# A decode kernel whose first loads are split over two DMA queues, and the same kernel with all loads on one

## The chip, the cores and the metric

The kernel runs on one core of one Trainium2 chip. The metric is the device time of one execution in microseconds, the median of several runs. A change of some microseconds out of 194 is what this case is about.

## The reference, cut to what matters

One token `x` (1 x 512) is normalised and goes into two branches. Branch A is attention over the last 4096 positions of a cache with 32 heads of 128; branch B is a small MLP. The output is `x + A * silu(B)`.

```python
xn = layernorm(x)
# A
q = xn @ wq                                   # 512 -> 32 heads x 128
k, v = k_cache[:, :, -4096:], v_cache[:, :, -4096:]
p = softmax((q . k) * 128 ** -0.5)
s = (p . v) @ wo                              # 4096 -> 512
# B (one token, so the shifted groups of gelu(...) are all zero)
x1 = xn + hs                                  # hs = 0 @ w2
g = silu(x1 + gelu(layernorm(x1) @ w3) @ w4)
return x + s * g
```

All tensors are bfloat16. The keys and the values are 33.6 MB each, wq and wo 4.19 MB each, w3 and w4 1.41 MB each, w2 0.52 MB; x is 1 KB.

## The kernel before, in words

The 32 heads are worked in eight groups of four (`G = 4`). A group's keys are one load of 4.19 MB (4096 KB in the profile's units: 128 partitions of 32 KB), its values another. `load()` (line 76) issues a load on SP's queue and keeps program order there; SP does nothing else. `load_kv` (lines 95 to 101) takes the next buffer of a pool and loads keys or values, in cuts where it is given some. Keys have three buffers, values two; a load waits on SP until the buffer's former contents have been read, and everything behind it on SP's queue waits with it.

The first part of the kernel, up to line 303, is the preparation. The layer norm of x is made from `x_bf` (x as 128 x 4, line 78); `x_row` (x as four rows, on partitions 0, 32, 64 and 96, line 80) serves the end of branch B (`xn_row`, line 242) and the last addition (line 653). The query weights `wq_sb` give the query in 32 matmuls (line 208), from which ScalarE and TensorE make the two forms that the groups use: `q_bc`, a row over all partitions (lines 214 and 216), and `q_pair`, columns (lines 221 and 225). Branch B is w2 (line 233, on zeros), w3 (20 matmuls of line 252 into `a_ps`), the gelu on ScalarE (`a_row`, line 255), a turn (`at_ps`, line 258; `a_bf`, line 260), w4 (lines 263 and 270 into `hr_ps`), VectorE's copy `hr` (line 273), the fold `h2_ps` (lines 275 and 276), `bv` on VectorE (line 278) and the silu (line 280). A scheduler orders this part on each engine by its own estimates, so an edit of the loads can change the order on TensorE, VectorE and ScalarE.

In the order of issue, ScalarE's queue has `x_bf`, `x_row` and wq; SP's has w2, w3, w4 in two pieces, then the keys.

The second part is a loop over `s` whose order on TensorE, VectorE and ScalarE is that of the program text (`manual_schedule`, line 527). In step `s` the keys of group `s` are worked and the values of group `s - 2`. Of a group's 128 key rows per partition, VectorE does 64 or 80 (`k_vector`, lines 317 to 323: a product `prod`, line 321, and a sum into `S`, line 323, in four parts); TensorE does the others (transposes, line 339, copied by ScalarE, line 342, then the scores, line 350). Softmax runs one step later; the values are wide matmuls (line 427), the last group's last cut a chain of 32 (line 461). The weights' pool `wts` is given back at `s == 2` (line 536) and its room becomes the values' buffers, so the first value load waits until the weights have been read. At the end, `wo` is applied in blocks (lines 518 and 155), and lines 651 to 654 make and store the output row (`out_row`, four partitions).

Of the kernel before, what the change touches and what calls it, by code (L numbers as in the profile page):

```python
# [8 lines left out]
P = 128  # L9
BF16 = mybir.dt.bfloat16  # L10
# [16 lines left out]
def kernel(  # L27
# [14 lines left out]
    nc = tc.nc  # L42

    Bb, Sq, D = A_x.shape
# [9 lines left out]
    KC = D // P  # L54
# [18 lines left out]
    wts = wts_guard.__enter__()  # L73

    def load(dst, src):
        return tc.keep_in_program_order(nc.sync.dma_start(out=dst, in_=src))  # L76

    x_bf = small.tile([P, KC], BF16, name="x_bf")
    nc.scalar.dma_start(out=x_bf[:], in_=A_x.rearrange("a b (p c) -> p (a b c)", p=P))
    x_row = small.tile([P, P], BF16, name="x_row")  # L80
    nc.gpsimd.memset(x_row[:], 0.0)
    nc.scalar.dma_start(out=x_row[0:P:32, :], in_=A_x.rearrange("a b (j n) -> (a b j) n", j=KC))
    wq_sb = wts.tile([P, KC, HD], BF16, name="wq_sb")
    nc.scalar.dma_start(out=wq_sb[:].rearrange("p c n -> p (c n)"),
                        in_=A_wq.rearrange("(a b c) n -> b a (c n)", a=4, c=KC))
    w2_sb = wts.tile([P, KC, D], BF16, name="w2_sb")
    load(w2_sb[:], B_w2.rearrange("(p c) n -> p c n", p=P))
    w3_sb = wts.tile([P, KC, F], BF16, name="w3_sb")
    load(w3_sb[:], B_w3.rearrange("(p c) n -> p c n", p=P))
    w4_sb = wts.tile([P, 11, D], BF16, name="w4_sb")  # L90
# [126 lines left out]
    for b in range(2):  # L217
# [5 lines left out]
        for t in range(2):  # L223
            rows = slice(64 * t, 64 * t + 64)
            nc.scalar.copy(out=q_pair[rows, 4 * b:4 * b + 4, :, G * t:G * t + G].rearrange("p g l a -> p g a l"),
                           in_=qt_ps[rows].bitcast(BF16).rearrange("p g (a m l) -> p g a m l", a=G, l=2)[:, :, :, 0, :])
# [38 lines left out]
    for i in range(11):  # L265
        n = P if i < 10 else 96
# [418 lines left out]
```

## Time and profile before

| What | us |
|---|---|
| median of three runs (193.26 to 193.96) | 193.93 |
| span of the profiled execution | 191.2 |
| VectorE busy in it | 150.9 (79%) |
| TensorE matmuls busy | 116.4 (61%) |
| ScalarE busy | 89.2 (47%) |
| wq: from issue to landing | 17.6 |
| w2: from issue to landing | 3.8 |
| x as columns: from issue to landing | 4.0 |
| query matmuls (L208) begin | 19.9 |
| first product of the keys (L321) begins | 26.1 |
| last of the values landed | 186.3 |

The profile is of one execution, and its times count from the start of its span. The page cuts the span into 40 equal slices and shows for each engine the busy share in tenths; the DMA row is the mean busy share of the 16 DMA engines, the row below it what they moved. "PEclk" is TensorE's granted clock in tenths. The queues are listed as q1 (SP's) and q10 (ScalarE's). The chain of waits follows the end of the execution back, at each step to what released it. In the timeline a row has start, length, engine, line, operation, and in brackets how long the engine had been idle and what ended that; "SPq" and "ACTq" are DMA issues on SP and ScalarE.

### The profile page before, as it was taken

The numbers are of one execution on the slowest core, as the hardware profiler recorded it, in microseconds if no ns is written. First come the engines' busy times: TensorE is split into PE (matmuls) and PEld (weight loads), VectorE is DVE, ScalarE is ACT, GpSimd is POOL, SyncE is SP. The second block draws the span as 40 slices with busy tenths as digits, with TensorE's granted clock in tenths as the row PEclk, the third lists the DMA queues.
The fourth block names the chain that finished last, engine by engine and source line by source line (L and its number), as shares of the span: only waits on it lengthen the run. The fifth ranks groups of instructions, "written<-read, shape, count | busy, mean of one in ns | idle before, by whom it ended". The sixth has DMA issues, their size and how long they took to land.

```text
span 191.2 us, 2839 instructions
## 1 busy us (share of the span) xinstructions
PE 116.4 (61%) x1159; PEld 74.2 (39%) x1159; DVE 150.9 (79%) x175; ACT 89.2 (47%) x191; POOL 2.3 (1%) x11
## 2 busy tenths in 40 slices
PE   1653754989825368256845772680888189739762
PEld 0430222767614334143334441540763077313322
DVE  1660159979999999999999999999999999980111
ACT  2001370888794076427464564542475148733120
POOL 2110000000000000000000000000000000000000
PEclk9999695555755557955695588557567858975998
DMA  6999999999999999999999999999999998999990
GB/s 211 447 430 404 431 418 439 439 439 437 432 434 439 432 429 432 432 439 432 422 432 432 418 422 418 452 439 435 439 432 434 435 432 372 471 425 405 420 371 32
DMA packets 4572, 79.02 MB, mean 413 GB/s; under 512 B 624, under 2 KB 1232, under 8 KB 1488
## 3 DMA queue, kind: packets, MB, share of 16 engines
q1 hardware_dynamic: 4264, 74.65, 91.6%
q10 hardware_dynamic: 296, 4.20, 5.1%
q8 instruction: 9, 0.15, 0.3%
q14 instruction: 3, 0.02, 0.0%
HBM read 78.84 MB, written 0.00 MB: 412 GB/s over the span
## 4 chain that ended last, share of the span: by engine, by line
DVE 46%; DMA 43%; PE 5%; ACT 3%; issue 1%; SPq 1%; ACTq 0%; DVEq 0%
DMA kv<-in_A_k_cache_dram 31%; DVE S L323 28%; DVE prod L321 15%; DMA kv<-in_A_v_cache_dram 10%; ACT kt L342 3%; DMA x_bf<-in_A_x_dram 2%; PE pt L339 2%; PE ov L427 1%; DVE m L366 1%; DVE S L364 1%; SPq L76 1%; PE sT L350 1%; DVE mx L374 1%; PE oT L461 1%; PE ot_ps L444 0%
## 5 line engine op out<-in xcount | busy, mean ns | idle before, releaser
L323 DVE TENSOR_REDUCE S<-prod 128x20 f32<-128x2560 bf16 (+1 forms) x32 | 86.0, 2686 | 1.1
L342 ACT COPY kt<-pt 128x1024 bf16<-128x1024 bf16 x52 | 51.2, 1013 | 40.4 <-PE pt L339 38.7
L339 PE MATMUL pt<-ident_f,kv 128*128 128x128 f32 x208 | 46.7, 376 | 10.8 <-DMA kv<-in_A_k_cache_dram 10.8
L321 DVE TENSOR_TENSOR prod<-kv,q_bc 128x2560 bf16<-128x2560 bf16 (+1 forms) x32 | 45.4, 1418 | 3.9 <-DMA kv<-in_A_k_cache_dram 3.7
L339 PEld LDWEIGHTS pt<-ident_f,kv 128*128 128x128 f32 x208 | 34.2, 196 | 14.4 <-DMA kv<-in_A_k_cache_dram 10.5
L350 PE MATMUL sT<-q_pair,kt 128*128 128x8 bf16 x416 | 19.4, 170 | 15.7 <-ACT kt L342 15.5
L350 PEld LDWEIGHTS <-kt 128*128 128x128 bf16 x416 | 16.4, 104 | 26.8 <-ACT kt L342 25.8
L427 PE MATMUL ov<-kv,pT 128*16 128x512 bf16 x248 | 22.0, 515 | 1.4 <-DMA kv<-in_A_v_cache_dram 1.4
L388 ACT ACTIVATE pT<-S,mb 128x128 bf16<-128x128 f32 x32 | 13.9, 573 | 0.3
L372 PE MATMUL mt_ps<-ident_f,m 128*1 128x128 f32 x8 | 2.9, 359 | 17.4 <-DVE rden L399 16.9
L433 ACT COPY ov_sb<-ov 128x512 f32<-128x512 f32 x8 | 4.7, 586 | 17.1 <-PE ov L427 17.1
L427 PEld LDWEIGHTS <-pT 128*16 128x16 bf16 x248 | 6.9, 109 | 13.2 <-issue 11.4
L359 ACT ACTIVATE own<-sT,par 128x48 f32<-128x48 f32 (+1 forms) x32 | 7.5, 356 | 3.7 <-PE sT L350 3.7
L444 PE MATMUL ot_ps<-ident_f,ov_sb 128*128 128x128 f32 x32 | 7.1, 359 | 2.9 <-ACT mb L384 1.9
L211 DVE CAST q_row<-qr_ps 128x512 bf16<-128x512 f32 x1 | 0.7, 692 | 9.9 <-PE qr_ps L208 9.9
L388 ACT ACTIVATION_READ_ACCUMULATOR pT<-S,mb 128x1 f32 x32 | 8.3, 258 | 0.0
L372 PEld LDWEIGHTS mt_ps<-ident_f,m 128*1 128x1 f32 x8 | 0.6, 80 | 17.9 <-DVE rden L399 17.2
L399 DVE RECIPROCAL rden<-den_ps 128x4 f32<-128x4 f32 x8 | 1.4, 175 | 7.0 <-PE den_ps L394 7.0
L381 PE MATMUL mb_ps<-md,par_t 5*128 5x4 f32 x16 | 3.9, 311 | 4.1 <-DVE md L376 4.1
L255 ACT ACTIVATE a_row<-a_ps 128x384 bf16<-128x384 f32 x1 | 0.5, 491 | 12.0 <-remote 12.0
L444 PEld LDWEIGHTS ot_ps<-ident_f,ov_sb 128*128 128x128 f32 x32 | 4.5, 178 | 3.9 <-ACT mb L384 2.3
L208 PE MATMUL qr_ps<-wq_sb,xq_bf 128*1 128x512 bf16 x32 | 3.1, 566 | 3.7 <-DMA wq_sb<-in_A_wq_dram 3.7
(122 smaller groups left out, 81.6 us busy)
## 6 DMA issues: line engine op xcount, KB each, us to landing
kv<-in_A_k_cache_dram SPq DMA_DIRECT2D x7, 4096.0 KB, 31.3
kv<-in_A_v_cache_dram SPq DMA_DIRECT2D x7, 4096.0 KB, 30.6
wq_sb<-in_A_wq_dram ACTq DMA_DIRECT2D x1, 4096.0 KB, 17.6
kv<-in_A_k_cache_dram SPq DMA_DIRECT2D x2, 2048.0 KB, 27.4
wo<-in_A_wo_dram SPq DMA_DIRECT2D x1, 2048.0 KB
kv<-in_A_v_cache_dram SPq DMA_DIRECT2D x1, 2048.0 KB
kv<-in_A_v_cache_dram SPq DMA_DIRECT2D x2, 1024.0 KB, 17.6
w_sb<-in_B_w_dram SPq DMA_DIRECT2D x1, 1376.0 KB, 9.1
```

Of the source, the lines that this page charges most:

```text
L321: nc.vector.tensor_tensor(out=prod[:, 0:m, :], in0=kn[:, rows, :], in1=q_bc[:, g:g + 1, :].to_broadcast([P, m, Dh]), op=ALU.mult)
L323: nc.vector.tensor_reduce(out=st[g]["S"][:, rows], in_=prod[:, 0:m, :], axis=AX.X, op=ALU.add)
L339: nc.tensor.transpose(pt[:, i, :], kn[:, c:c + 2, :].rearrange("p c d -> p (c d)").bitcast(FP32), ident_f[:])
L342: nc.scalar.copy(out=kts[b][:, 0:n, :], in_=pt[:, 0:n, :].bitcast(BF16))
L350: nc.tensor.matmul(st[g]["sT"][:, c:c + 2, :].rearrange("p c a -> p (c a)"), lhsT=kt[:, i, l::2], rhs=q_pair[:, g, l, :], start=(l == 0), ...
L359: nc.scalar.mul(s["own"][:, 0:m, a], s["sT"][:, 0:m, a], par[:, a:a + 1])
L372: nc.tensor.transpose(mt_ps[:], s["m1"][:], ident_f[:])
L381: nc.tensor.matmul(mb_ps[:], lhsT=par_t[:].rearrange("k b a -> k (b a)"), rhs=md[:], start=True, stop=True)
L388: nc.scalar.activation(out=s["pT"][:, :, a], in_=s["S"][:], func=ACT.Exp, scale=scale, bias=mb[:, a:a + 1], accum_out=s["sum"][:, a:a + 1])
L427: nc.tensor.matmul(ov[r:r + 4 * G], lhsT=s["pT"][:, c:c + 4, :].rearrange("p i a -> p (i a)"), rhs=v[:, c:c + 4, :], start=(i < 4), stop=( ...
L433: nc.scalar.copy(out=s["ov_sb"][:], in_=ov[:])
L444: nc.tensor.transpose(ot_ps[:, step * j:step * j + P], s["ov_sb"][:, j, :], ident_f[:])
```

## The change

The three loads on ScalarE's queue go to SP's through `load()`, which also keeps them in program order there, and w2's load is put ahead of them. SP's order is now w2, x as columns, x as rows, wq, w3, w4 in two pieces, keys. ScalarE issues no DMA any more. Everything after w3's load is unchanged in the text.

```diff
     def load(dst, src):
         return tc.keep_in_program_order(nc.sync.dma_start(out=dst, in_=src))
 
+    w2_sb = wts.tile([P, KC, D], BF16, name="w2_sb")
+    load(w2_sb[:], B_w2.rearrange("(p c) n -> p c n", p=P))
     x_bf = small.tile([P, KC], BF16, name="x_bf")
-    nc.scalar.dma_start(out=x_bf[:], in_=A_x.rearrange("a b (p c) -> p (a b c)", p=P))
+    load(x_bf[:], A_x.rearrange("a b (p c) -> p (a b c)", p=P))
     x_row = small.tile([P, P], BF16, name="x_row")
     nc.gpsimd.memset(x_row[:], 0.0)
-    nc.scalar.dma_start(out=x_row[0:P:32, :], in_=A_x.rearrange("a b (j n) -> (a b j) n", j=KC))
+    load(x_row[0:P:32, :], A_x.rearrange("a b (j n) -> (a b j) n", j=KC))
     wq_sb = wts.tile([P, KC, HD], BF16, name="wq_sb")
-    nc.scalar.dma_start(out=wq_sb[:].rearrange("p c n -> p (c n)"),
-                        in_=A_wq.rearrange("(a b c) n -> b a (c n)", a=4, c=KC))
-    w2_sb = wts.tile([P, KC, D], BF16, name="w2_sb")
-    load(w2_sb[:], B_w2.rearrange("(p c) n -> p c n", p=P))
+    load(wq_sb[:].rearrange("p c n -> p (c n)"), A_wq.rearrange("(a b c) n -> b a (c n)", a=4, c=KC))
     w3_sb = wts.tile([P, KC, F], BF16, name="w3_sb")
     load(w3_sb[:], B_w3.rearrange("(p c) n -> p c n", p=P))
```

## The prediction

> **What bounds the kernel now.** I read the 40 slices first, then the DMA queues, then the chain of waits, and last the start of the span in short windows. The slices:
>
> ```profile
> span 191.2 us, 2839 instructions
> ...
> DVE  1660159979999999999999999999999999980111
> ...
> PEclk9999695555755557955695588557567858975998
> DMA  6999999999999999999999999999999998999990
> GB/s 211 447 430 404 431 418 439 439 439 437 432 434 439 432 429 432 432 439 432 422 432 432 418 422 418 452 439 435 439 432 434 435 432 372 471 425 405 420 371 32
> DMA packets 4572, 79.02 MB, mean 413 GB/s; under 512 B 624, under 2 KB 1232, under 8 KB 1488
> ## 3 DMA queue, kind: packets, MB, share of 16 engines
> q1 hardware_dynamic: 4264, 74.65, 91.6%
> q10 hardware_dynamic: 296, 4.20, 5.1%
> ...
> DVE 46%; DMA 43%; PE 5%; ACT 3%; issue 1%; SPq 1%; ACTq 0%; DVEq 0%
> ```
>
> The DMA row stands at 8 or 9 from the second slice to the 39th. q1 (SP) and q10 (ACT: x twice and wq, 4.20 MB) together fill 96.7% of all 16 engines over the whole span. The last row, of the chain of waits, names VectorE for 46%, but that is a trap: the chain follows a key load back to the VectorE step that released its buffer, and the engines were still busy with older loads then. VectorE waits for data in its turn (the row at 41.91 below). So the time is: first packet, then 79 MB at what the engines give, then a short tail. An idle microsecond of the DMA engines anywhere moves the end by one microsecond; work elsewhere counts only if it starves the queue. The windows (last two columns: DMA share and GB/s; packets are counted where they start, so short windows exceed 1) and the issues:
>
> ```profile
> 0.00:1.50 1.50, 0.52 (x1) 0.10 (x1) 0.52 (x6) 0.00 (x0) 0.94 (x8) 1.00 0.00 0
> 1.50:2.00 0.50, 0.09 (x1) 0.00 (x0) 0.00 (x0) 0.00 (x0) 0.29 (x2) 1.00 0.96 115
> 2.00:2.50 0.50, 0.00 (x0) 0.00 (x0) 0.00 (x0) 0.00 (x0) 0.00 (x0) 1.00 0.47 139
> 2.50:3.00 0.50, 0.00 (x0) 0.00 (x0) 0.00 (x0) 0.04 (x1) 0.00 (x0) 1.00 0.95 254
> 3.00:3.50 0.50, 0.00 (x0) 0.00 (x0) 0.00 (x0) 0.50 (x1) 0.00 (x0) 1.00 0.94 320
> 3.50:4.00 0.50, 0.00 (x0) 0.00 (x0) 0.00 (x0) 0.50 (x1) 0.00 (x0) 1.00 1.35 508
> ```
> ```profile
> 0.73 1.81 SPq L76 DMA_DIRECT2D w_sb<-in_B_w_dram  x4
> 0.74 0.40 ACTq L79 DMA_DIRECT2D x_bf<-in_A_x_dram  x1
> 1.18 1.11 ACTq L82 DMA_DIRECT2D x_row<-in_A_x_dram  x1
> 2.32 0.61 ACTq L84 DMA_DIRECT2D wq_sb<-in_A_wq_dram  x1
> ...
> 41.91 1.49 DVE L321 TENSOR_TENSOR prod<-kv,q_bc 128x2560 bf16<-128x2560 bf16 x1 [0.99 <-DMA kv<-in_A_k_cache_dram]
> ...
> 188.68 0.66 SPq L76 DMA_DIRECT2D out_dram<-out_row  x1
> ```
>
> The six windows add up to 0.67 MB at 4.0 us; w2 alone is 0.52 MB, which they reach at about 3.7. From 4 to 186 the rate is 423 to 433 GB/s. The first x bytes land 4.0 us after their issue.
>
> **The change, part by part.** The span is 191.2; the median of the three runs is 193.93, so 2.7 lies around the span, and I carry that over. All sums are differences to it.
>
> *Start of the queue.* Now SP issues w2, w3, w4 one after another (0.45 each), so w3's descriptors wait long before w2 is out. Afterwards SP issues w2 (0.73 to 1.18), x as columns (0.40, the ACT row), x as rows (1.11 by the ACT row; 0.66 by the other transfer of four partitions, out_row on SP), then wq. wq's issue thus starts at 2.24 to 2.69. From the start of an issue to its first packet, the trace's packet records have 1.0 us for w2 (0.73 to 1.74) and 1.6 for x as columns (0.74 to 2.35). wq's first bytes come at 3.2 to 4.3. w2's last packet lies at 3.4 to 3.7: at 3.7 if it goes as now, at 3.4 if w2 gains by not sharing turns with 128 packets of 8 bytes. Ends: a gain of 0.3 (w2 out at 3.4, wq there in time) and a loss of 0.9 (4.3 less 3.4). I take a loss of 0.2: the short issue (0.66) is SP's own row, and 1.3 us from issue to first packet lies midway, so wq starts at 3.55 to 4.0 against 3.6. The cover is w2's two microseconds of transfer; without it the three issues, 0.40 + 1.11 + 0.61 = 2.1, would all be idle time.
>
> The Trainium skill's page "DMA: Bandwidth & Descriptors" (section Specifications) gives 0.6 us to the first byte for SP's and ScalarE's path, less than the 1.0 and 1.6 above. By it wq would be in the engines by 3.3, there would be no gap, and the sum would be 193.6 to 193.9; the rows here are longer, and I go by them.
>
> *The bytes.* Same 79 MB, same packets (wq's are of 32 KB, as the keys' are). In front of the first half of group 0's keys stand the same 7.5 MB in either order, so those keys still land at 26 us plus the gap. One queue does not slow them: between 42 and 130 us only SP's loads run, at 433 GB/s, against 426 from 8 to 20 us where both queues had work. Cost 0.
>
> *ScalarE.* It loses 2.1 us of issues and gains one table load (in the order in which the changed kernel's build lists each engine's instructions, three stand ahead of the keys' copies instead of two; 1.28 us each). ScalarE idles 12.0 us before L255 and 5.1 before L210, so the load is hidden. Cost 0.
>
> *TensorE and VectorE.* wq now lands at about 14.2 instead of 19.9 (3.65 + 4.19 MB at 425 GB/s, + 0.7 to the semaphore), w3 at 17.5 instead of 10.3, w4 at 20.9. The listed order now mixes L252's 20 matmuls into the query chain, and VectorE's copy hr (L273) and bv (L278) stand ahead of the first product L321 instead of between products. Worked out: a_ps done by 17.5 + 2.9 (L252) + 2.0 (the query's L214 and L221 between) = 22.4; a_row 0.5, at_ps and a_bf 0.5, the 16 matmuls of L263 and L270 1.6, hr 0.7, then to the end of bv 1.3 (as 30.2 to 31.6 now): 27.0. The first product starts at 27.0 instead of 26.1. But 0.96 (0.68 + 0.28) leaves the stretch behind it, which now runs from 26.1 to 40.9, so VectorE is done at 40.9 as before, ahead of group 1's keys (the row at 41.91, with 0.99 idle). Cost 0. With that cover gone, VectorE releases key buffers later and SP's issues queued behind the release (keys, then values, in program order) come later; that costs only once the queue runs dry. The shallowest place I find is the last values: issued from 166.8 on, 4.19 MB, landed at 186.3; they need 9.7 us of transfer, so some 9.8 us of older work lay ahead.
>
> *Waits.* The semaphores the first key loads wait for belong to w2 and the two x loads, all landed by some 5 us; 20 MB are then queued. The first value load waits for the weights' buffers (31.19 now) and gets them about 4 us earlier. Nothing is late by it.
>
> Sum: +0.2 + 0 + 0 + 0 + 0, **194.1 us**.
>
> **Rivals.**
> *A longer gap at the start.* The same place at its upper end: x as rows costs SP its 1.11 and wq's first packet takes 1.6 us: 193.9 + 0.9 = 194.8, past that with another few tenths of issue. For it: ACT's issue really took 1.11. Against: two engines were issuing then, here one.
> *The small loads hold the queue.* If a queue starts no packet before the preceding transfer is complete, each x load costs what out_row takes from the end of its issue to the end of the span, 191.2 - 188.68 - 0.66 = 1.9; two make 3.7, so 197.6. It decides from the moment completion, not packets, occupies the engines. Against: w2, w3, w4 and the first keys stand in one queue now with the share at 0.94 to 1.01.
> The skill's same page ("Rules for kernel authors") says that transfers under 64 KB are mostly overhead; with the fixed 2.0 us that its section "Anatomy of one DMA" states (for GpSimd's path) the two would cost 4.0 and the time would be 197.9. The trace does not bear it out as engine time.
> *VectorE sets the pace after all,* as the chain says: then taking hr and bv out of the product stretch gains 0.96, so 193.0. Against: the 0.99 idle and the full DMA row.
> *Clock in the tail.* After the last landing at 186.33 TensorE's two groups (L461 0.96, L155 0.39) ran at clock 1.0; PEclk is 5 in about half of all slices. If the moved work shifts a half-clock stretch onto the end: +1.4, so 195.5 with the 0.2. Against: PEclk reads 9, 9 and 8 in the last three slices.
> That the change does not do what it says is excluded: the listed order has no DMA left on ScalarE.
>
> **How the numbers follow.** About 0.5% (1 us) is what a measurement of this kernel can tell from no change. Forecast 0.77; longer gap (194.8 and up) 0.10, about half of it beyond 194.9; held queue 0.04; clock 0.05; VectorE 0.04. Faster takes the VectorE case and a little of the start's gain with the runs' own scatter (193.26 to 193.96): 0.06. Slower takes held queue, clock, half the longer gap and 0.03 for loss in the forecast's own upper end: 0.17. Same: 0.77. The range runs from the gain of 0.3 below the lower runs' middle, 193.2, to the loss of 0.9 with a little scatter, 195.1; clock and held queue lie above it, VectorE's case just below.
>
> **What would show it.** In the profile after: wq's issue on SP near 2.3 to 2.7; the windows from 3.5 to 4.5 with a GB/s dip of no more than some tenths of a microsecond's worth; wq landed near 14; the first product near 26 to 27; VectorE again idle before group 1's keys; the DMA row at 9 throughout; the last values landing within 0.5 of 186.3. I am wrong if the DMA row shows a hole after w2, if group 1's keys no longer come after VectorE is done and the queue runs dry later, or if the rate of the one queue falls under 425 in the first 20 us.

## The result and the profile after

The change made the kernel slower: median 194.93 us (194.67 to 195.68, four runs) against 193.63 (193.26 to 193.96, four runs) before, a ratio of 1.0082 (95% interval 1.0065 to 1.0100). The profiled execution has a span of 192.6 us against 191.2. The page of the changed kernel, with the rows that answer to those of before:

```profile
span 192.6 us, 2840 instructions
...
DVE  1560129999999999999999999999899998980111
...
PEclk9999997579555556955585579558555858975995
DMA  7899999999999999999999999999999999999990
GB/s 218 367 404 422 413 432 463 422 429 427 429 430 435 435 418 422 429 435 435 432 435 429 435 432 418 452 435 425 435 435 437 418 435 395 463 435 398 415 364 14
...
q1 hardware_dynamic: 4560, 78.84, 96.3%
...
DVE 54%; DMA 29%; PE 10%; ACT 4%; issue 2%; SPq 1%; POOL 1%; ACTq 0%; POOLq 0%
```

The row to look at is GB/s. Its second slice reads 367 where before had 447, its third 404 for 430. Times the slice (4.815 us here, 4.78 before), the first three slices moved 4.76 MB in 14.4 us; before they had moved 5.20 in 14.3. The missing 0.44 MB take 1.0 us at 433 GB/s, and that is most of the 1.3 us. The same page says how much of it is empty time and how much slow packets: q1's 96.3% of 192.6 are 185.5 us of work of 16 engines; before, 96.7% (q1 and q10 together) of 191.2 were 184.9. The same bytes took 0.6 us longer in the engines, and the engines stood empty about 0.5 us longer.

The trace's packet records, summed into a curve of bytes over time, say where. The changed kernel is 0.18 us ahead of before at 0.5 MB (w2 came out quicker), 0.60 behind at 0.8 MB, 0.85 at 1 MB, 0.99 at 2 MB, and then 1.12 at 8, 20, 50 and 78 MB. Everything was lost in the first 8 us and nothing was given back or lost later.

The issues on SP (start and length in us, then line, tile and source):

```profile
0.73 0.39 SPq L76 DMA_DIRECT2D w_sb<-in_B_w_dram  x1
1.18 0.41 SPq L76 DMA_DIRECT2D x_bf<-in_A_x_dram  x1
1.64 0.67 SPq L76 DMA_DIRECT2D x_row<-in_A_x_dram  x1
2.36 0.60 SPq L76 DMA_DIRECT2D wq_sb<-in_A_wq_dram  x1
3.00 1.53 SPq L76 DMA_DIRECT2D w_sb<-in_B_w_dram  x3
```

wq is issued at 2.36, within the forecast 2.24 to 2.69, and x as rows took 0.67, the short price. Now the windows behind w2 (window, length, busy time on PE, PEld, DVE, ACT and POOL, clock, DMA share, GB/s):

```profile
3.50:4.00 0.50, 0.00 (x0) 0.00 (x0) 0.00 (x0) 0.00 (x0) 0.00 (x0) 1.00 1.78 463
4.00:4.50 0.50, 0.00 (x0) 0.00 (x0) 0.17 (x1) 0.00 (x0) 0.00 (x0) 1.00 2.52 655
4.50:5.00 0.50, 0.45 (x2) 0.45 (x2) 0.00 (x0) 0.00 (x0) 0.00 (x0) 1.00 0.00 0
5.00:5.50 0.50, 0.14 (x1) 0.05 (x1) 0.29 (x2) 0.00 (x0) 0.00 (x0) 1.00 0.00 0
5.50:6.00 0.50, 0.00 (x0) 0.00 (x0) 0.42 (x3) 0.00 (x0) 0.00 (x0) 1.00 1.39 590
```

A zero here is not an idle engine: a packet is counted where it starts, and a 32 KB packet normally fills an engine for 1.22 us. Two empty windows in a row say that all engines are inside one packet each for a full microsecond or more. By the packet records w2's last packet starts at 3.64, wq's first on the 16 engines between 3.78 and 4.50 (1.4 to 2.1 us after the start of its issue), and those 16 take 1986 ns in the mean; the next 16 take 1237. So the loss behind w2, called the hole from here on, has two parts: 0.54 us of idle engines (mean of the 16, from 2 to 7 us; 0.06 before), and a first round 0.77 us too long. Against them stand some 0.3 us that w2's own packets were quicker.

The rest of the trace, from wq's landing to the end, and behind it two rows of before to compare with:

```profile
15.54 3.58 PE L207 MATMUL qr_ps<-wq_sb,xq_bf 128*1 128x512 bf16 x32 [3.45 <-DMA wq_sb<-in_A_wq_dram]
28.63 1.22 DVE L320 TENSOR_TENSOR prod<-kv,q_bc 128x2048 bf16<-128x2048 bf16 x1
42.95 1.49 DVE L320 TENSOR_TENSOR prod<-kv,q_bc 128x2560 bf16<-128x2560 bf16 x1
187.65 0.99 PE L460 MATMUL oT<-pT,kv 128*128 128x4 bf16 x32 [0.16 <-DMA kv<-in_A_v_cache_dram]
188.88 0.60 PE L154 MATMUL y_ps<-wo_rows,o 128*1 128x128 bf16 x16 [0.25 <-DVE o L470]
190.18 0.60 SPq L76 DMA_DIRECT2D out_dram<-out_row  x1
```
```profile
26.09 1.23 DVE L321 TENSOR_TENSOR prod<-kv,q_bc 128x2048 bf16<-128x2048 bf16 x1 [2.19 <-DMA kv<-in_A_k_cache_dram]
...
186.38 0.96 PE L461 MATMUL oT<-pT,kv 128*128 128x4 bf16 x32 [0.17 <-DMA kv<-in_A_v_cache_dram]
187.59 0.39 PE L155 MATMUL y_ps<-wo_rows,o 128*1 128x128 bf16 x16 [0.26 <-DVE o L471]
```

The first product starts 2.54 us later than before and group 1's product no longer waits for keys: here the trace offers a second story, that VectorE is late and holds the key buffers. But the last matmuls still wait for the last values (the bracket at 187.65) and start 1.27 later than before (187.65 for 186.38); that is the bytes' 1.1 and little else. Another 0.2 of the 1.5 at the output's issue is clock: the last 16 matmuls of L154 took 0.60 instead of 0.39, at a granted clock of 0.50 in that window where before had 1.00.

### The profile page after: what moved, and what is told of

It reads as the page before. It is cut to its first block, busy times and chain, and to the rows that moved or that the text cites. A ratio compares the mean times of both kernels' runs of the same rounds, so it can differ in the third digit from the quotient of the medians.

```text
span 192.6 us, 2840 instructions
## 1 busy us (share of the span) xinstructions
PE 119.7 (62%) x1159; PEld 74.7 (39%) x1159; DVE 151.3 (79%) x175; ACT 90.5 (47%) x192; POOL 2.3 (1%) x11
## 3 DMA queue, kind: packets, MB, share of 16 engines
q1 hardware_dynamic: 4560, 78.84, 96.3%
## 4 chain that ended last, share of the span: by engine, by line
DVE 54%; DMA 29%; PE 10%; ACT 4%; issue 2%; SPq 1%; POOL 1%; ACTq 0%; POOLq 0%
DVE S L322 33%; DVE prod L320 17%; DMA kv<-in_A_k_cache_dram 12%; DMA kv<-in_A_v_cache_dram 10%; DMA wq_sb<-in_A_wq_dram 7%; PE pt L338 2%; ACT kt L341 2%; PE qr_ps L207 2%; PE ov L426 1%; PE sT L349 1%; DVE m L365 1%; DVE S L363 1%; SPq L76 1%; ACT L254 1%; PE a_ps L251 1%
## 5 line engine op out<-in xcount | busy, mean ns | idle before, releaser
L426 PE MATMUL ov<-kv,pT 128*16 128x512 bf16 x248 | 23.0, 532 | 1.2 <-DMA kv<-in_A_v_cache_dram 1.2
L209 ACT CAST q_row<-qr_ps 128x512 bf16<-128x512 f32 x1 | 0.6, 586 | 15.4 <-PE qr_ps L207 15.4
L380 PEld LDWEIGHTS mb_ps<-md,par_t 5*128 5x128 f32 x16 | 3.8, 291 | 6.0 <-PE sT L349 4.6
L207 PE MATMUL qr_ps<-wq_sb,xq_bf 128*1 128x512 bf16 x32 | 3.6, 625 | 3.5 <-DMA wq_sb<-in_A_wq_dram 3.5
```

Source lines behind the costliest of these rows:

```text
L207: nc.tensor.matmul(qr[b][32 * a:32 * a + 1], lhsT=xq_bf[:, c:c + 1], rhs=wc[:, 4 * b:4 * b + 4, a, :], start=False, stop=(c == KC - 1), sk ...
L380: nc.tensor.matmul(mb_ps[:], lhsT=par_t[:].rearrange("k b a -> k (b a)"), rhs=md[:], start=True, stop=True)
L426: nc.tensor.matmul(ov[r:r + 4 * G], lhsT=s["pT"][:, c:c + 4, :].rearrange("p i a -> p (i a)"), rhs=v[:, c:c + 4, :], start=(i < 4), stop=( ...
```

## The experiments

**Theory A** is the hole behind w2. **Theory B** is VectorE's late start, through key buffers that come free later. Each kernel's edit is against the changed kernel unless it says against before; every ratio is to the kernel before, run on the same chip.

### Which of the two: x on ScalarE's queue, w3 ahead, late products, the change again

`x_on_act` takes the two small loads out of SP's queue and leaves the changed order of work:

```diff
-    load(x_bf[:], ...)
+    nc.scalar.dma_start(out=x_bf[:], in_=...)
-    load(x_row[0:P:32, :], ...)
+    nc.scalar.dma_start(out=x_row[0:P:32, :], in_=...)
```

> Only the two small x loads go back to ScalarE's queue; w2, wq, w3, w4 stay on SP's, and VectorE keeps the order of the changed kernel (hr and bv ahead of the first product). Theory A (the loss is a hole in the DMA engines behind w2, while SP issues the x loads, together with a slow first round of wq's packets): wq is issued 1.1 us sooner, right behind w2, no hole, so the ratio to before is 1.000 to 1.002 (193.6 to 194.0). Theory B (the loss comes from VectorE's later first product, which releases every key buffer a microsecond later): the order is unchanged, so 1.008 (194.9) stays.

Measured: 193.67, ratio 1.0030 (1.0006 to 1.0055). SP's first issues and VectorE's first product in its timeline:

```profile
0.73 0.39 SPq L76 DMA_DIRECT2D w_sb<-in_B_w_dram  x1
1.18 0.63 SPq L76 DMA_DIRECT2D wq_sb<-in_A_wq_dram  x1
...
27.58 1.23 DVE L320 TENSOR_TENSOR prod<-kv,q_bc 128x2048 bf16<-128x2048 bf16 x1
```

With wq issued at 1.18 its packets are there when w2 ends (3.69 to 4.34), the engines idle 0.01 us, the first round takes 1251 ns, and the bytes are 0.15 us behind before instead of 1.12. VectorE starts 1.5 us late all the same. The ratio lies just above theory A's 1.002 and well under theory B's 1.008; this kernel's runs scatter more than the others (193.33 to 196.48, seven of twelve up to 193.7).

`w3_ahead` keeps one queue and moves w3's tile and load in front of the x loads:

```diff
     load(w2_sb[:], ...)
+    w3_sb = wts.tile([P, KC, F], BF16, name="w3_sb")
+    load(w3_sb[:], B_w3.rearrange("(p c) n -> p c n", p=P))
     x_bf = small.tile([P, KC], BF16, name="x_bf")
...
-    w3_sb = wts.tile([P, KC, F], BF16, name="w3_sb")
-    load(w3_sb[:], B_w3.rearrange("(p c) n -> p c n", p=P))
```

> All loads on SP, w3 moved ahead of the two x loads: w2, w3, x, x, wq, w4. Theory A: w3's 1.41 MB (3.3 us of transfer) cover the issues of x and wq, no hole, ratio 1.000 to 1.002 (193.6 to 194.0), although x lands some 3 us later. Theory B: hr and bv still stand ahead of the first product, 1.008 (194.9). A third view, that one queue is slower than two in itself: 1.008 as well.

Measured: 193.50, ratio 1.0004 (0.9995 to 1.0013). Its windows where the changed kernel has its hole:

```profile
4.00:4.50 0.50, 0.00 (x0) 0.00 (x0) 0.00 (x0) 0.00 (x0) 0.00 (x0) 1.00 1.16 440
4.50:5.00 0.50, 0.00 (x0) 0.00 (x0) 0.00 (x0) 0.00 (x0) 0.00 (x0) 1.00 0.78 330
5.00:5.50 0.50, 0.00 (x0) 0.00 (x0) 0.00 (x0) 0.00 (x0) 0.00 (x0) 1.00 1.10 462
```

And from its timeline wq's issue, the first product and the last matmuls of the values:

```profile
2.85 0.60 SPq L76 DMA_DIRECT2D wq_sb<-in_A_wq_dram  x1
...
29.26 1.22 DVE L320 TENSOR_TENSOR prod<-kv,q_bc 128x2048 bf16<-128x2048 bf16 x1
...
186.60 0.95 PE L460 MATMUL oT<-pT,kv 128*128 128x4 bf16 x32
```

wq is issued later still, at 2.85, but w3's 1.4 MB keep the engines busy until 7.1 us. wq's first round takes 1217 ns, and the whole loss is gone although the first product (29.26) is later than in the changed kernel. Only the missing bracket at 186.60 says that compute has come level with the bytes at the end. One queue is not what costs; what stands in it behind a short load does.

`late_products`, against before, repeats group 0's first product, so that VectorE runs late while the loads stay as they were:

```diff
+        for _ in range(3 if g == 0 and part == 0 else 1):
             nc.vector.tensor_tensor(out=prod[:, 0:m, :], ...)
```

> The kernel before with the first product of group 0 done three times (the result is the same): VectorE is 2.46 us later through group 0, so that it no longer waits for group 1's keys and releases the key buffers some 1.4 us later, as much as in the changed kernel or more; the loads are untouched. Theory A: nothing, ratio 0.999 to 1.001. Theory B: 1.005 to 1.008 (194.6 to 195.1).

Measured: 193.57, ratio 1.0006 (0.9991 to 1.0021). From its timeline, group 0's tripled product and group 1's first:

```profile
26.09 3.75 DVE L322 TENSOR_TENSOR prod<-kv,q_bc 128x2048 bf16<-128x2048 bf16 x3 [1.50 <-DMA kv<-in_A_k_cache_dram]
...
43.48 1.49 DVE L322 TENSOR_TENSOR prod<-kv,q_bc 128x2560 bf16<-128x2560 bf16 x1
```

Group 1's product comes at 43.48, without a wait and later than the changed kernel's 42.95, and nothing is lost. Theory B falls, at this lateness. The chain of waits, which rose from 46% to 54% VectorE with the change, pointed the wrong way: it reads 72% VectorE in `late_products` and 71% in `w3_ahead`, which lost nothing.

`changed_again` is the changed kernel a second time, on another chip.

> The changed kernel itself, so that the next three stand beside it on one chip: ratio to before 1.0065 to 1.010, as measured first. All theories agree.

Measured: 194.63, ratio 1.0064 (1.0044 to 1.0085), bytes 1.26 behind, idle 0.33, first round 2043 ns. The idle part is smaller here and the slow round longer.

### What sets the hole: when wq is issued, or how small the loads are

`one_more_small` and `three_more_small` put one or three more loads like x as rows ahead of wq:

```diff
+    x_row2 = small.tile([P, P], BF16, name="x_row2")
+    load(x_row2[0:P:32, :], A_x.rearrange("a b (j n) -> (a b j) n", j=KC))
```

> The changed kernel with one more load of x as rows (into a tile that nothing reads) ahead of wq on SP. Theory A: the hole grows by the issue of one such load, 0.67 us, so 1.0035 above the changed kernel, 1.0117 to before (195.6 to 195.9). Theory B: wq lands only 0.7 later, the queue is deep, 1.008 to 1.010.

> The changed kernel with three more loads of x as rows (into tiles that nothing reads) ahead of wq on SP; one more had put the bytes 0.3 us later than the changed kernel's, not 0.67. If the hole is what costs, and one more load cost less because the first round of wq's packets got faster as the hole grew (it can only get faster once), three more put wq's issue 1.9 us later and the whole of the two further loads shows: bytes 2.6 us behind before's, ratio 1.013 to 1.015 (196.0 to 196.4). If the loss is not the hole but the mere fact of a restart behind an empty queue, it stays at 1.008 to 1.010.

Measured: 194.88, ratio 1.0078 (1.0064 to 1.0092) with one, and 196.12, 1.0139 (1.0118 to 1.0160) with three. Three cost the time that was expected, with bytes 2.14 us behind instead of the expected 2.6; the windows of `three_more_small` show a real hole, two windows in which next to nothing starts after w2's 4 KB packets:

```profile
4.00:4.50 0.50, 0.00 (x0) 0.00 (x0) 0.00 (x0) 0.00 (x0) 0.00 (x0) 1.00 0.06 5
4.50:5.00 0.50, 0.09 (x1) 0.09 (x1) 0.17 (x1) 0.00 (x0) 0.00 (x0) 1.00 0.01 2
```

One more cost less than theory A expected (1.0117), just under what theory B gave: the idle time rose by 0.5 us, to 1.06, but the first round was only 1754 ns. The price of an issue is not simply added; the slow first round shrinks as the idle time grows.

`x_row_later` issues wq ahead of x as rows, `x_cols_on_act` takes only x as columns (128 pieces of 8 bytes) off SP's queue:

```diff
-    load(x_row[0:P:32, :], ...)
     load(wq_sb[:]...)
+    load(x_row[0:P:32, :], ...)
```
```diff
-    load(x_bf[:], ...)
+    nc.scalar.dma_start(out=x_bf[:], in_=...)
```

> All loads on SP: w2, x as columns, wq, x as rows, w3, w4. wq is issued at 1.64 instead of 2.36, so its packets are in the queue by about 3.0, before w2 is out at 3.6. Theory of the hole: hole and slow first round both go, ratio 1.000 to 1.002 (193.5 to 193.9). If the slow first round of wq belongs to its large packets or to SP issuing beside it, not to the empty queue, half of the loss stays: 1.003 to 1.005.

Measured: 195.36, ratio 1.0099 (1.0079 to 1.0119), a miss. wq is issued at 1.64, 0.7 us earlier, and yet its packets start at 3.88 to 4.99. Its timeline has the issue,

```profile
1.64 0.63 SPq L76 DMA_DIRECT2D wq_sb<-in_A_wq_dram  x1
```

and its windows the hole, 131 GB/s where the engines give 430:

```profile
4.00:4.50 0.50, 0.00 (x0) 0.00 (x0) 0.00 (x0) 0.00 (x0) 0.00 (x0) 1.00 0.31 131
```

That suggested **theory P**: the 128 small pieces ahead of wq in the queue hold it, not the moment of issue (**theory I**). `x_cols_on_act` and `x_cols_twice` were made to tell these apart.

> Only x as columns (128 pieces of 8 bytes) goes back to ScalarE's queue; SP has w2, x as rows (4 pieces), wq, w3, w4. wq is issued at about 1.85, later than the 1.64 of the kernel with x as rows behind wq, which still had the hole. Theory I (the moment of issue decides, and 2.2 to 3.3 us pass to the first packets): hole and slow first round stay, ratio 1.006 to 1.010. Theory P (the queue's work per piece decides: the 128 small pieces between w2 and wq hold up wq's descriptors, whenever wq is issued): no hole, 1.000 to 1.003.

Measured: 195.09, ratio 1.0083 (1.0062 to 1.0104). wq is issued at 1.91, without any 8-byte piece ahead of it on SP's queue, and the hole is there: packets from 3.83 to 4.47, idle 0.42, first round 1900 ns. Theory P falls, for the 8-byte pieces; x as rows still stands between w2 and wq here.

```diff
+    x_bf2 = small.tile([P, KC], BF16, name="x_bf2")
+    load(x_bf2[:], A_x.rearrange("a b (p c) -> p (a b c)", p=P))
```

> The changed kernel with x as columns loaded twice (once into a tile that nothing reads), both ahead of wq. Theory I: wq is issued 0.41 later, so at most 0.4 us more than the changed kernel: 1.007 to 1.010. Theory P: 128 more small pieces cost the queue about as much as the first 128 did, 1 us: 1.012 to 1.014.

Measured: 195.94, ratio 1.0130 (1.0113 to 1.0147), which looked like theory P after all. But its bytes were 1.14 us behind at 2 MB and 1.83 at 78: it lost time on the way, as none of the kernels above does. The new tile, small as it is, moves the buffers behind it, the values' among them, by 32 bytes. `x_cols_twice_256` is the same load into a tile of 256 bytes, and `pad_32_more` is the changed kernel with its unused tile made 32 bytes longer:

```diff
+    x_bf2 = small.tile([P, P], BF16, name="x_bf2")
+    load(x_bf2[:, 0:KC], ...)
```
```diff
-    small.tile([P, 96], BF16, name="pad")
+    small.tile([P, 112], BF16, name="pad")
```

> The changed kernel with x as columns loaded twice, the second time into a tile of 256 bytes per partition, so that every later buffer moves by 256 bytes and not by 32 as in the run before. Theory I (the moment of wq's issue decides; 0.41 later): 1.007 to 1.010 to before. Theory P (128 more small pieces hold the queue up): 1.012 to 1.014 as before.

> The changed kernel with an unused tile made 32 bytes longer, which moves the value buffers, wo's and the softmax tiles by 32 bytes; nothing else differs. If the place of the buffers is what made the packets 0.3% longer in the run with x as columns twice (there the bytes fell 0.55 us further behind from 46 us on, and the products 1 to 2 us at the end): 1.010 to 1.013. If not: 1.0065 to 1.010, as the changed kernel.

Measured: `x_cols_twice_256` 194.78, ratio 1.0070 (1.0053 to 1.0087), bytes 1.31 behind at 2 MB and 1.19 at 78; so a second load of 128 pieces costs no more than one of four pieces (1.0078), and theory P falls again. `pad_32_more` 196.02, ratio 1.0128 (1.0112 to 1.0144), with the same instructions as the changed kernel. Its page:

```profile
span 194.0 us, 2840 instructions
...
q1 hardware_dynamic: 4560, 78.84, 95.9%
```

95.9% of 194.0 are 186.0 us of engine work, 0.6 more than the changed kernel's 185.5. From 46 us on its 32 KB packets took 1219 to 1223 ns (means over stretches of 20 us), the changed kernel's 1213 to 1220, and its bytes fall another 0.56 us behind between 20 and 78 MB. That is not all of its loss: at 20 MB it was 1.63 us behind already, where the changed kernel's two traces have 1.12 and 1.26, so the hole itself scatters from run to run.

The kernels side by side. "First packets" is when the first 32 KB packet started on the first and on the last of the 16 engines, "first round" the mean of those 16, "idle" the mean idle time of the engines from 2 to 7 us, "lag" the time by which 20 MB came later than in before's trace:

| kernel | wq issued | first packets | idle us | first round ns | lag us | ratio |
|---|---|---|---|---|---|---|
| `x_on_act` | 1.18 | 3.69-4.34 | 0.01 | 1251 | 0.15 | 1.0030 |
| `x_row_later` | 1.64 | 3.88-4.99 | 0.60 | 1730 | 1.35 | 1.0099 |
| `x_cols_on_act` | 1.91 | 3.83-4.47 | 0.42 | 1900 | 0.89 | 1.0083 |
| the change | 2.36 | 3.78-4.50 | 0.54 | 1986 | 1.12 | 1.0082 |
| `changed_again` | 2.36 | 3.99-4.38 | 0.33 | 2043 | 1.26 | 1.0064 |
| `x_cols_twice_256` | 2.83 | 4.29-5.16 | 1.23 | 1694 | 1.19 | 1.0070 |
| `one_more_small` | 2.91 | 4.35-5.31 | 1.06 | 1754 | 1.43 | 1.0078 |
| `three_more_small` | 4.00 | 5.40-6.31 | 1.94 | 1667 | 2.14 | 1.0139 |
| `w3_ahead` | 2.85 | 7.13-7.41 | 0.14 | 1217 | -0.19 | 1.0004 |
| `pad_32_more` (buffers moved) | 2.36 | 3.88-5.44 | 0.94 | 1941 | 1.63 | 1.0128 |
| `x_cols_twice` (buffers moved) | 2.83 | 4.29-4.99 | 0.59 | 1701 | 1.28 | 1.0130 |

Issued at 2.36 or later behind w2, wq gets its first packet 1.4 to 1.6 us after the start of its issue, and its first round is over, in the mean of the 16, after 3.4 to 4.0 us. So from there on theory I holds, and the two parts are one price: in `three_more_small` eight of the first packets start at 5.40 to 5.47 and take about 2.0 us, eight at 6.13 to 6.31 and take 1.2 to 1.4, and all end between 7.39 and 7.64. Issued at 1.64 or 1.91 the first packet comes no earlier than issued at 2.36 (w2's last packets end only at 3.8 to 4.0), and the last engines still wait to 4.99 and 4.47. There theory I fails too, and what holds them stays open. One reading is untested: only `x_on_act` has no small load between w2 and wq, so that any small load there, and not the moment of issue, may be what delays wq.

### wq alone on ScalarE's queue

```diff
-    load(wq_sb[:]...)
+    nc.scalar.dma_start(out=wq_sb[:]..., in_=...)
```

> Only wq goes back to ScalarE's queue, where it is issued at 0.74; w2, both x loads, w3, w4 stay on SP's, and VectorE has the order of the kernel before. The queue of ScalarE holds wq from about 2 us on, so the engines have work while SP issues the small loads: no hole, ratio 1.000 to 1.003. If the small loads themselves cost engine time in SP's queue, 1.004 or more.

Measured: 195.93, ratio 1.0127 (1.0107 to 1.0147), a miss, and not by the hole: its bytes run 0.2 to 0.4 us ahead of before all the way. Its page has, in the chain of waits by engine,

```profile
DVE 70%; PE 15%; DMA 7%; issue 4%; ACT 1%; POOLq 0%; POOL 0%; ACTq 0%; SPq 0%; DVEq 0%
```

and its timeline

```profile
14.36 0.17 DVE L183 CAST x_f<-x_bf 128x4 f32<-128x4 bf16 x1 [13.02 <-DMA x_bf<-in_A_x_dram]
...
29.27 1.23 DVE L321 TENSOR_TENSOR prod<-kv,q_bc 128x2048 bf16<-128x2048 bf16 x1 [0.16 <-ACT q_bc L216]
...
189.25 0.95 PE L461 MATMUL oT<-pT,kv 128*128 128x4 bf16 x32
```

x as columns, 1 KB, landed 9.7 us later than the 4.7 of before. Each engine has eight of its 8-byte pieces, and between two of them a 32 KB packet of wq goes out from the other queue: 8 times 1.22 is 9.8. The whole preparation starts late, VectorE's last key maximum (L374) comes at 175.72 instead of 171.17, and the last matmuls no longer wait for values. Here a late VectorE does cost, though not through the key buffers as theory B has it, for the loads are not late: compute itself ends last. 4.5 us late costs about 2.4, where 1.9 us (`w3_ahead`, 173.08, and `late_products`, 173.00) cost nothing. The Trainium skill's page "DMA: Bandwidth & Descriptors", section "Queues, rings and completion order", says that each engine goes round its queues by packets; the trace agrees, with 9.7 us for eight turns, each with a single 8-byte piece in it.

### Without w2

If the time is bytes, w2's 0.52 MB should be worth 1.2 us at 433 GB/s. `no_w2_two_queues` is before without w2's load and its products with zeros, `no_w2_one_queue` the same with all loads on SP, w3 first:

```diff
-    w2_sb = wts.tile([P, KC, D], BF16, name="w2_sb")
-    load(w2_sb[:], ...)
...
-    xc3, _, rstd3 = ln_stats(x1_f[:], "z3")
+    xc3, _, rstd3 = ln_stats(xn_f[:], "z3")
...
-    terms = [(shifted_bf[:, c:c + 1], w2_sb[:, c, :]) for c in range(KC)]
+    terms = []
```

> The kernel before without w2's load and without its two products, which multiply zeros (the output stays the same). If the engines' work sets the end here, 0.52 MB at 433 GB/s less is 1.2 us: ratio 0.9935 to 0.995 (192.3 to 192.6). If VectorE or TensorE sets it: 1.000.

> The same left out (w2's load and its products with zeros), all loads on SP, w3 first, then x, x, wq, w4, keys. w3 covers the small loads, so no hole. In the kernel with w2, w3, x, x, wq, w4 the last values no longer made TensorE wait, so compute was about level with the loads: if the query's and branch B's work follow the loads forward, 0.994 to 0.996; if VectorE's chain now sets the end, 0.998 to 1.001.

Measured: 192.95 both, ratios 0.9978 (0.9968 to 0.9988) and 0.9977 (0.9968 to 0.9987), less than half of the 1.2 us. The small tiles that went away had moved the later buffers by 64 bytes, and the packets were longer again: from 46 us to the end their mean is 1219.8 and 1219.5 ns, before's 1216.6. The `_256` kernels lengthen the unused tile by those 64 bytes (`[P, 96]` to `[P, 128]`).

> The kernel before without w2's load and its products with zeros (the output stays the same), with the unused tile longer by 64 bytes, so that the value buffers lie where they did before. If their place cost the 0.7 us that the first try lost on the way: 0.9935 to 0.9955 (192.1 to 192.5). If not: 0.998 again.

> The same left out, all loads on SP with w3 first, value buffers where they were before. As with two queues if one queue costs nothing once w3 covers the small loads: 0.9935 to 0.9965. If the restart behind an empty queue shows here too: 0.998 to 1.000.

Measured: 192.37, ratio 0.9941 (0.9925 to 0.9957), and 192.27, ratio 0.9931 (0.9915 to 0.9948). The page of `no_w2_one_queue_256`:

```profile
span 190.2 us, 2796 instructions
...
q1 hardware_dynamic: 4416, 78.32, 96.7%
```

The 0.52 MB are worth 1.0 and 1.1 us, and the intervals hold the 1.2, with two queues or with one; the mean packet is back at 1216.2 and 1216.0 ns. One queue, with a long load first and without w2, is level with two queues without w2, and faster than both before and after.

## Why the prediction was wrong, step by step

**What bounds the kernel: right.** The DMA engines do. Every kernel but `wq_on_act` follows the lag of its bytes to some 0.8 us (median against one trace), and w2's bytes gave back their time.

**Start of the queue: the step that failed.** The prediction took +0.2, with +0.9 as its far end. Its first half held: wq's issue at 2.36 (forecast 2.24 to 2.69), x as rows at 0.67, the first packet 1.42 us after the issue (forecast 1.0 to 1.6, taken 1.3), w2 out at 3.64 to 3.8. Two things were not in it. It compared the first packet with w2's end, but there are 16 engines, and the last got its first packet at 4.50, 2.1 us after the issue; the mean idle time is 0.54. And it priced only idle time: the slow first round, 1986 ns for 1217, adds 0.77. No row that it showed has a large load start behind an empty queue, but before's packet records hold a hint: the first 16 of w2's 4 KB packets, which found the engines empty, took 548 ns in the mean, the later half 174. With w2's 0.3 to the good the parts make some 1.0 of the 1.12 us by which the bytes lag, five times the term. The first sign that the prediction named for being wrong, a hole after w2, is there in the windows. Its own rival "a longer gap at the start", 194.8 and up with a chance of 0.10, is what happened, but by another way than it said: it had asked for an issue of 1.11 for x as rows, which took 0.67, and it knew nothing of the slow round.

The Trainium skill's 0.6 us to the first byte ("DMA: Bandwidth & Descriptors", section Specifications) is too short as a price from the start of an issue to the packet: 1.04 for w2 into an empty machine, 1.42 to 2.14 for wq. Counted from the end of the issue (1.12 and 2.96) w2's is 0.65, which agrees, and wq's 0.82 to 1.54, which does not. The Trainium skill's rule in the same page's section "Issuing engines are not separate DMA queues" is that several issuing engines save only the time it takes to issue, which is usually small beside the DMA; `w3_ahead` agrees, 1.0004 with one queue. The changed kernel is the case in which that small time is not hidden.

**The bytes: right.** The lag is 1.12 at 8 MB and at 78 MB. The rate from 8 to 20 us is 417 GB/s, under the 425 that the prediction had set as its alarm, yet the curve of bytes shows no loss there: a window of 12 us is a poor measure where packets are counted by their start. `x_on_act` reads 403 there and loses nothing in it.

**ScalarE: the size was off, the cost to the end nothing.** The added table load is not hidden by idle time. It stands at 23.22 to 24.50, because copies of the query fill ScalarE just before, and a_row starts some 0.5 us after its matmuls are done.

**TensorE and VectorE: right on the cost, wrong on the cover.** The first product was forecast at 27.0 and came at 28.63: the hole's 1.1 and that table load. VectorE was not done ahead of group 1's keys (42.95, no wait). That cost nothing because the queue is deep, the second cover that the prediction named; `late_products` shows it.

**Rivals.** Held queue: no; `three_more_small` lags 2.14 us and the change 1.12, so a further small load costs 0.34, not 1.9. VectorE as the pace: no. Clock in the tail: the profiled execution has a slow last block of matmuls, worth 0.2, not 1.4.

**The base.** The prediction started from 193.93, the median of three runs. Over the later comparisons before ran at 193.40 to 193.57, so about 0.4 of the base was scatter, and the miss in the difference (1.3 for 0.2) is larger than the miss in the time (194.93 for 194.1). The range, to 195.1, held the time because its upper end was this rival's; that the forecast time came so near owes something to a base that was too high, which is luck.

## What to carry to other kernels

Where the DMA engines set the time, look at what each queue has in the engines while the next load is issued: a short first load must cover all issues up to the next large one and some 1.4 to 2.4 us more (first engine to last, in these kernels), or a longer load belongs in front. Price a queue that runs empty by the idle time and by the slow first round behind it, over all 16 engines, not by the first packet. A chain of waits that names an engine is no proof; delay that engine and see. Before an edit of small tiles is read as an effect of loads, see that it has not moved the large buffers.

## What the runs showed of the hardware

A large load issued behind a short one starts slowly: the first packets of 32 KB took 1667 to 2043 ns in the mean of the 16 engines, against 1217 to 1251 where a load covered them (the table above). Not every engine is slow: in `x_row_later` the seven that start by 4.04 took 1213 to 1262 ns and the other nine 2020 to 2247; in `one_more_small` the four that start last took 1211 to 1213. The first round gets shorter as the idle time gets longer because the early packets end no sooner than the late ones; what they wait for is not settled.

A small load beside a large one on the other queue waited a whole large packet for each of its pieces: 1 KB in 128 pieces landed at 14.4 us instead of 4.7 (`wq_on_act`).

The place of the buffers matters. With the values' buffers where before has them, or 256 or 768 bytes further, packets of 32 KB took 1216.0 to 1216.8 ns in the mean from 46 us to the end; moved by 32 or 64 bytes, in four kernels, 1219.5 to 1220.2. That is 0.3%, some 0.55 us over the last 58 MB. The whole difference is 0.4% of the kernel without w2 (0.9978 against 0.9941, the bytes alike at 20 MB) and 0.5 to 0.6% of the changed one (1.0128 against 1.0082 and 1.0064), where part of it is the longer hole at the start. What makes these places better stays open; other distances were not tried.
